# Chunk 1 of a fused mLSTM and feed-forward kernel: the next step's preparation handed over behind the joint products

## The chip, the core and the metric

The kernel runs on one core of one Trainium2 chip. The metric is device time in microseconds (us). The core has a matrix engine (TensorE, PE in the profile, with its weight loads shown apart as PEld), a vector engine (VectorE, DVE), a scalar engine (ScalarE, ACT), a general engine (GpSimd, POOL) and a sequencer that only issues transfers here (SyncE, SP). Each engine works through its own instructions in a fixed order and waits where one of them needs something that is not there yet. Transfers between memory and the on-chip buffers are issued by a queue and run beside the engines.

## The reference

Two blocks are computed, one after the other, in float32. The first is an mLSTM cell over 4 batches, 8 heads, 768 tokens and a head width of 40. At each token a decayed matrix state takes in one outer product, and the query reads it:

```python
m_new = np.maximum(f_gate[:, :, t] + m, i_gate[:, :, t])
C = f_stab * C + i_stab * einsum('bhd,bhe->bhde', vt, kt)
n = f_stab * n + i_stab * kt
h_tilde = einsum('bhde,bhe->bhd', C, qt)
y[:, :, t] = sigmoid(o_gate[:, :, t]) * h_tilde / maximum(abs(n . qt), 1.0)
```

The second takes y as 3072 tokens of width 320 through a feed-forward pair: `h = x @ w_in` (320 to 2048), `g = maximum(0.01 * h, h)`, `g @ w_out` (2048 to 320). The two weight matrices arrive as 64-bit floats and are narrowed to 32 bits on the chip.

## The kernel before, in words

The 768 tokens are cut into 6 chunks of 128. A step `s` is one chunk of one batch, so that chunk c holds steps 4c to 4c+3. In this document **step 4 to step 7** are the four steps of chunk 1, which alone the change touches. The recurrence inside a chunk is replaced by matrix products over two halves of 64 tokens, with one carried state per batch, kept in `S_t[s % 4]`.

The first chunk is written out (`first_chunk`). From then on a loop runs the feed-forward units of the chunk before (`ffs`, line 946 on) and sets the cell's work of the current chunk between them. In chunk 1 there are 30 units, i = 0 to 29. Units 0 to 13 are halves of the first product (line 743, `ph`, about 2.25 us of PE each), and units 14 to 29 are quarters of the second (line 778, `po`, about 2.2 us each). The tuple `place` (line 940) says behind which unit each of the cell's pieces stands. For the steps 4 to 7 there are two pieces, or visits:

- `u_parts(s)`, the first visit: it turns the scaled query (`split_qs`, line 504, `tq`), finishes the exponentials that are left, and makes the joint products, which are the scores and the state's increments in one pair of PSUM banks `sd0` and `sd1` (lines 598 and 603). VectorE then multiplies the scores by the decays (line 608, `qn`) and adds the first increment (line 580).
- `u_plain(s)`, the second visit, three units later: `prep_o` (line 478), the values `hN` (line 649), on POOL the decay of the state's second half (`state_next(s, 1)`, line 576), on VectorE the denominators and the gate (lines 617 to 660), on POOL the product at line 665, and on VectorE the second increment (`state_add(s, 1)`, line 580).

They stand behind units 2 and 5 for step 4, 7 and 10 for step 5, 12 and 15 for step 6, 18 and 21 for step 7. Behind unit 16 stands `u_gates(2)` (lines 312 and 317, `tg`).

The preparation of a step is `ahead(s)` (line 821). For the steps of chunk 1 it issues, in this order: `u_split(s)`, which turns the keys and the queries on PE (64 small products at line 518 into the PSUM pair `tk0`, `tk1`) and copies them out on ACT (four copies, line 524, `kqT`); the list of eight exponentials (line 442), of which three are run with each following unit; `prep_qs(s)` on POOL (line 471, `y<-rb`); the load of the queries of step s + 2 on SP (line 366, or line 382 and the spread of line 405 from step 8 on); `state_next(s, 0)` (line 576) and `prep_vu(s)` (line 462) on POOL; and `prep_mask(s + 1)` on POOL (line 434, `w<-w,i`), which adds the causal mask to the decays `w` of the step after.

What `ahead(s)` reads arrives by transfers of the SP queue: the keys (line 340, `kn`), the values (line 343), the decays (line 397, `w<-a_dr`, two transfers), the queries (line 366, `rb<-in_q_dram`) and the output gates. The order of that queue is fixed when the program is built. SP gives its transfers eight completion counters in turn, so that each issue first waits until the transfer eight places ahead of it has landed. Between them stand the loads of the weights (lines 213 and 218).

Meanwhile `narrow_weights` (lines 231 to 247) narrows the remaining weights, one operation on ACT and six on VectorE for each piece, some with each unit.

PSUM is given out in two groups of four banks: `mm` for `ph` and `po`, and `c` for the cell's pieces (`tq`, `tk`, `sd`, `hN`, `tg`). A piece gets a bank when the piece that held it has been read.

The order on PE, VectorE, ACT and POOL is that of the calls, since the whole runs under a manual schedule.

Of the kernel before, what the change touches and what calls it, by code (L numbers as in the profile page):

```python
# [18 lines left out]
def kernel(  # L19
# [27 lines left out]
    B, H, S, D = q.shape  # L47
# [140 lines left out]
    def load_weights(n):  # L188

        m = n - QN  # L190
        if n < QN:
            dst = w_in[:, n, :]
        else:
            dst = w_out[:, 2 * m : 2 * m + 2, :].rearrange("p a d -> p (a d)")
        to = dst
        if wide:
            if n < 2:
                at = NF * GT - 2 * WC * (n + 1)
                raw = acts_l[:, at : at + 2 * WC].bitcast(U64)
            elif n < QN:  # L200
                raw = raw_t[:, WC * (n - 2) : WC * (n - 1)]
            elif m < 2:
                raw = w_out[:].rearrange("p f d -> p (f d)")[:, (2 + m) * WC : (3 + m) * WC].bitcast(U64)
            else:
                at = (4, 0, 1, 2, 3, 4)[m - 2] * HW
                raw = raw_t[:, at : at + HW]
            raws[n] = (raw, dst)
            to = raw
        if n < QN:
            src = moe_w_in[:, n * QC : (n + 1) * QC].rearrange("(k p) (r c) -> r p k c", p=DP, r=2)  # L210
            for slot in range(KC):
                for r in range(2):
                    nc.sync.dma_start(  # L213
                        to[DP * r : DP * (r + 1), 2 * P * slot : 2 * P * (slot + 1)], src[r, :, SLOTS[r][slot], :],
                    )
        else:
            rows = moe_w_out[2 * m * P : 2 * (m + 1) * P, :]
            nc.sync.dma_start(to.rearrange("p (a d) -> p a d", d=Dm), rows.rearrange("(a p) d -> p a d", p=P))
# [142 lines left out]
    def load_late(s, i):  # L361

        if B <= s < 2 * B:
            if i > 0:
                c, b = divmod(s, B)
                nc.sync.dma_start(natural(s, i), (k, q, o_gate)[i][b, :, ts(c, P), :].rearrange("h p d -> p h d"))
        elif s < NS:
            load_blocks(s, i)
# [60 lines left out]
    def prep_mask(s):  # L429
        if s in masked:  # L430
            return
        masked.add(s)
        w = st[s]["w"]
        nc.gpsimd.tensor_tensor(w, w, cm2.unsqueeze(1).to_broadcast([P, H, SL]), op=ALU.add)  # L434
# [367 lines left out]
    def cell_units(c):  # L802
        if c == 1:
            units = [(fn, c * B + n) for n in range(B) for fn in (u_parts, u_plain)]
            units.insert(2 * B - 2, (u_gates, c + 1))
            return units + [(u_x, s) for s in range(B, 2 * B)]
        units = [(fn, c * B + n + m) for n in range(0, B, 2) for fn in (u_parts, u_mix) for m in range(2)]
        if c + 1 < NB:
            units.insert(2 * B - 2, (u_gates, c + 1))
        return units  # L810
# [5 lines left out]
    def run(steps, n=None):  # L816

        for _ in range(H if n is None else n):
            next(steps, None)
# [23 lines left out]
    def feed(s):  # L843
        load(s)
        spread(s)

    def first_chunk():

        for n in range(B):
            load(n)  # L850
        load_o(0)
        load_o(1)
        load_weights(0)
        load_o(2)
        load_o(3)
        for n in range(1, 3):
            load_weights(n)
        gates(0)
        gates_exp(0)
        warm(14)  # L860
        bu, a, _ = bus[0]
        gates_T(0, bu)
        u_transpose(0)
        spread_first(a, 0)
        run(prep_exp(0))
        prep_vu(0)
        prep_vu(1)
        prepare_tiles()
        u_transpose(1)
        u_scores(0)  # L870
        u_state(0)
        run(prep_exp(1))
        spread_first(a, 2)
        gates(1)
        gates_exp(1)
        u_scores(1)
        u_values(0)
        u_state(1)
        u_transpose(2)
        prep_o(0)  # L880
        gate(0)
        run(prep_exp(2))
        prep_vu(2)
        w = narrow_weights(0)
        next(w, None)
        u_values(1)
        u_gates(1)
        u_scores(2)
        prep_o(1)
        gate(1)  # L890
        u_state(2)
        for _ in w:
            pass
        u_transpose(3)
        run(prep_exp(3))
        prep_vu(3)
        prepare_step(0)
        prepare_step(1)
        u_x(0)
        u_values(2)  # L900
        u_scores(3)
        u_x(1)
        u_state(3)
        prep_o(2)
        gate(2)
        w = narrow_weights(1)
        for _ in range(4):
            next(w, None)
        ffs = ff_units(0)
        ffs[0]()  # L910
        u_values(3)
        prep_o(3)
        gate(3)
        u_x(2)
        ffs[1]()
        for _ in w:
            pass
        u_x(3)
        prepare_step(2)
        prepare_step(3)  # L920
        return ffs

    E = mybir.EngineType
    with tc.manual_schedule(engines={E.PE, E.DVE, E.Activation, E.Pool}):
        ffs = first_chunk()
        for s in (B, B + 1):
            feed(s)
            for i in range(1, 3):
                load_late(s, i)
            if s == B:  # L930
                load_weights(3)
        for n in range(3):
            load_weights(QN + n)
        for s in (B + 2, B + 3):
            feed(s)


        ffs = ffs[2:]
        fetch = {4: (3, 4), 8: (5, 6), 15: (7,)}
        place = (2, 5, 7, 10, 12, 15, 16, 18, 21, 22, 24, 26, 28)  # L940
        late = {}
        masks = {0: (2, 3), 12: (4, 5)}
        pairs = (2, 2, 6, 6, 14, 14, 19, 19, 19)
        now = (None for n in range(2, QN + NF // 2) for _ in narrow_weights(n))
        for c in range(1, NB + 1):
            if c > 1:
                ffs = ff_units(c - 1)
            cells = cell_units(c) if c < NB else []
            n_ff, n_c = len(ffs), len(cells)
            done = fed = 0  # L950
            waiting = []
            for i in range(n_ff):
                if c == 1:
                    run(now, 2 if i < 10 else 3 if i < 14 else 4)
                    for n in fetch.get(i, ()):
                        load_weights(QN + n)
                    if i == 0:
                        prep_mask(B)
                        ahead(B)
                        load_fi(3)  # L960
                for s, steps in lazy.items():
                    if s in late and late[s] > 0:
                        late[s] -= 1
                    else:
                        run(steps, 3)
                for n in masks.get(i, ()) if 1 < c < NB else ():
                    if c * B + n < NS:
                        prep_mask(c * B + n)
                ffs[i]()
                if c + 1 < NB:  # L970
                    if i == (1 if c == 1 else 0):
                        gates(c + 1)
                    if i == (3 if c == 1 else 2):
                        gates_exp(c + 1)
                upto = min(n_c, sum(p <= i for p in (place if c == 1 else pairs)))
                while done < upto:
                    fn, s = cells[done]
                    fn(s)
                    done += 1
                    if fn is u_mix:  # L980
                        waiting.append(s)
                    if fn is u_plain and s < 2 * B - 1 or fn is u_parts and s == 2 * B - 1:
                        ahead(s + 1)
                    elif fn is u_mix:
                        ahead(s + 2)
                    elif fn is u_plain:
                        prep_mask(s + 2)
                        ahead(s + 2)
                if i >= n_ff // 2 - 1:
                    for s in waiting:  # L990
                        gather_x(s)
                    waiting.clear()
                while fed < done:
                    fn, s = cells[fed]
                    fed += 1
                    if fn in (u_mix, u_plain):
                        load_late(s + NR, 2)
                        if s + NL < NS:
                            feed(s + NL)
# [31 lines left out]
```

## Time and profile before

| | |
|---|---|
| median of 3 runs | 528.49 us (528.32 to 528.70) |
| the profiled execution's own time | 528.25 us |
| its span, first to last instruction | 526.4 us |
| PE busy | 513.2 us (97%) |
| DVE, ACT, POOL busy | 240.3, 168.1, 113.0 us |
| mean granted PE clock | 0.976 |

The profile covers one execution. Its span is 1.85 us shorter than that execution's time, and its time is 0.24 us below the median. Times in the lines are from the start of the span. A line of the timeline gives start, length, engine, source line, operation and output<-inputs; a bracket at its end tells how long the engine sat idle before it and what ended that. SPq is the issuing of a transfer, and its length is that of the issue, not of the transfer.

### The profile page before, as it was taken

To read this page: it belongs to the slowest core of one execution; us is meant where nothing else is said; L and a number is where in the kernel's file an instruction comes from. 1 tells how busy PE (TensorE), PEld (TensorE's weight loads), DVE (VectorE), ACT (ScalarE), POOL (GpSimd) and SP (SyncE) were. 2 spreads that over 40 slices of the span, in tenths; PEclk is the share of its full clock that TensorE was granted. 3 is DMA by queue.
4 is the path that set the end of the run, shared out by engine and by line. 5 is a ranking of instruction groups with operands and counts; after the bars stand their busy time and mean duration, and the time that the engine had idled before them with its cause. 6 is when DMAs were issued, how large, how long until landed. Compare 5 with 4: busy or idle time off the path is not lost.

```text
span 526.4 us, 11333 instructions
## 1 busy us (share of the span) xinstructions
PE 513.2 (97%) x4501; PEld 336.3 (64%) x4501; DVE 240.3 (46%) x431; ACT 168.1 (32%) x458; POOL 113.0 (21%) x145
## 2 busy tenths in 40 slices
PE   8889989999999999999999999999999999999997
PEld 7877878777555577555577555577554577544675
DVE  4679998999328446028445028344028230000000
ACT  4565865534534212034212124212125100122100
POOL 4244354152205121015021015021013010000000
PEclk9668999999999999999999999999999999999999
DMA  9977687888755626685626676626542112000000
GB/s 116 156 204 153 138 212 171 196 145 175 146 137 105 137 72 150 129 174 107 138 75 143 134 150 129 138 76 155 125 102 52 50 52 87 14 0 1 12 12 25
DMA packets 165284, 59.13 MB, mean 112 GB/s; under 512 B 128816, under 2 KB 156016, under 8 KB 165232
## 3 DMA queue, kind: packets, MB, share of 16 engines
q1 hardware_dynamic: 164848, 58.28, 51.0%
q8 instruction: 35, 0.57, 0.5%
q10 hardware_dynamic: 384, 0.13, 0.1%
q14 instruction: 17, 0.14, 0.1%
HBM read 51.68 MB, written 6.70 MB: 111 GB/s over the span
## 4 chain that ended last, share of the span: by engine, by line
PE 83%; SPq 6%; DVE 4%; DMA 2%; ACT 2%; issue 1%; POOL 1%; ACTq 0%; POOLq 0%
PE po L778 38%; PE ph L743 36%; PE pT L679 3%; SPq L213 3%; PE sd L598 3%; SPq L338 2%; SPq L352 1%; PE sd L603 1%; DMA rb<-in_q_dram 1%; DVE raw L245 1%; DVE qn L608 1%; DMA S<-in_v_dram 0%; DMA raw<-in_moe_w_in_dram 0%; PE tk L518 0%; PE hN L649 0%
## 5 line engine op out<-in xcount | busy, mean ns | idle before, releaser
L743 PE MATMUL ph<-xT,w_in 64*128 64x512 f32 (+1 forms) x1120 | 215.2, 536 | 0.6 <-ACT acts L751 0.6
L778 PE MATMUL po<-w_out,acts 128*128 128x320 f32 x768 | 211.1, 434 | 0.0
L778 PEld LDWEIGHTS po<-w_out,acts 128*128 128x128 f32 x768 | 144.5, 190 | 62.6 <-issue 4.1
L743 PEld LDWEIGHTS ph<-xT,w_in 64*128 64x128 f32 x1120 | 107.8, 189 | 94.4 <-issue 87.7
L751 ACT ACTIVATE acts<-ph 128x512 f32<-128x512 f32 (+1 forms) x112 | 53.9, 534 | 151.8 <-PE ph L743 151.7
L608 DVE TENSOR_TENSOR qn<-w,sd 64x512 f32<-64x512 f32 x40 | 27.4, 684 | 97.7 <-PE sd L603 57.1
L576 POOL TENSOR_TENSOR S<-S,f 40x336 f32<-40x336 f32 x36 | 30.9, 858 | 101.9 <-PE pT L679 65.8
L442 ACT ACTIVATE w<-w,gT 128x64 f32<-128x64 f32 (+1 forms) x192 | 51.1, 348 | 3.1 <-POOL w L434 2.1
L434 POOL TENSOR_TENSOR w<-w,i 128x512 f32<-128x512 f32 x20 | 28.1, 1411 | 104.7 <-ACT bu L294 53.0
L786 ACT COPY y<-po 128x320 f32<-128x320 f32 x12 | 5.1, 423 | 83.3 <-PE po L778 83.3
L786 ACT COPY hn<-po 128x320 f32<-128x320 f32 x12 | 5.1, 426 | 76.0 <-PE po L778 76.0
L686 DVE STREAM_TRANSPOSE hb<-pT 128x512 f32<-128x512 f32 x16 | 11.4, 714 | 39.2 <-PE pT L679 39.0
L495 DVE TENSOR_TENSOR qn<-kqT,ea 64x512 f32<-64x512 f32 x32 | 27.3, 854 | 0.9
L693 POOL TENSOR_TENSOR xb<-xb,den 128x320 f32<-128x320 f32 x16 | 11.7, 728 | 66.5 <-DVE xb L690 66.5
L598 PEld LDWEIGHTS sd<-kqT 40*64 40x64 f32 x640 | 19.9, 135 | 6.1 <-issue 6.1
L697 DVE STREAM_TRANSPOSE x<-xb 128x512 f32<-128x512 f32 x16 | 18.1, 1130 | 7.7 <-POOL xb L693 7.7
L598 PE MATMUL sd<-kqT 40*64 40x64 f32 x640 | 21.5, 220 | 0.0
L603 PE MATMUL sd<-S,vu 64*40 64x42 f32 x576 | 20.1, 214 | 0.7 <-POOL vu L462 0.7
L489 DVE STREAM_TRANSPOSE kqT<-rb 128x512 f32<-128x512 f32 x32 | 20.5, 677 | 0.0
L603 PEld LDWEIGHTS sd<-S,vu 64*40 64x40 f32 x576 | 18.6, 111 | 0.8 <-POOL vu L462 0.8
L580 DVE TENSOR_TENSOR S<-S,sd 40x336 f32<-40x336 f32 x36 | 18.1, 503 | 1.0
L679 PEld LDWEIGHTS pT<-qn,S 128*64 128x64 f32 x512 | 15.6, 138 | 3.6 <-issue 3.5
(126 smaller groups left out, 364.9 us busy)
## 6 DMA issues: line engine op xcount, KB each, us to landing
w<-a_dr SPq DMA_DIRECT2D x40, 128.0 KB
rb<-in_k_dram SPq DMA_DIRECT2D x64, 80.0 KB
rb<-in_q_dram SPq DMA_DIRECT2D x64, 80.0 KB
rb<-in_o_gate_dram SPq DMA_DIRECT2D x64, 80.0 KB
ea<-a_dr SPq DMA_DIRECT2D x32, 128.0 KB
kn<-in_k_dram SPq DMA_DIRECT2D x24, 160.0 KB
raw<-in_moe_w_out_dram SPq DMA_DIRECT2D x6, 640.0 KB
S<-in_v_dram SPq DMA_DIRECT2D x80, 40.0 KB
```

Of the source, the lines that this page charges most:

```text
L434: nc.gpsimd.tensor_tensor(w, w, cm2.unsqueeze(1).to_broadcast([P, H, SL]), op=ALU.add)
L442: yield nc.scalar.activation(w[:, h, :], w[:, h, :], AF.Exp, bias=gT[c][:, 0, bh : bh + 1], scale=1.0)
L489: nc.vector.transpose(d["kqT"][:, i].rearrange("p (h t n) -> p h n t", n=TS, t=QW), raw_blocks(s, i, QW).rearrange("p (h n) d -> p h n d", ...
L495: nc.vector.tensor_tensor(mixed(s)[rows, 1 - r], d["kqT"][rows, 1].rearrange("p (h t) -> p h t", t=SL), d["ea"][rows], op=ALU.mult,)
L576: nc.gpsimd.tensor_tensor(new, old, g, op=ALU.mult)
L598: nc.tensor.matmul(bank[1 - u][toks, h, :], lhsT=kqT[rows, 0, ts(h, SL)], rhs=kqT[rows, 1, ts(h, SL)], start=True, stop=True,)
L603: nc.tensor.matmul(dC[u][:, h].rearrange("p k d -> p (k d)"), lhsT=d["ku"][toks, h], rhs=S_v[s % NL][toks, u, h, :, :V1], start=True, stop ...
L608: nc.vector.tensor_tensor(mixed(s)[toks, u], w[toks], bank[1 - u][toks], op=ALU.mult)
L679: nc.tensor.matmul(pT[DP * r : DP * (r + 1), j * P + u * SL : j * P + (u + 1) * SL], lhsT=S[:, u, h, :], rhs=m[:, u, h, :], start=True, st ...
L743: nc.tensor.matmul(ph[r][:, cols], lhsT=w_row(r, slot, j), rhs=xT[DP * r : DP * (r + 1), slot, cols], start=(slot == 0), stop=(slot == KC ...
L751: nc.scalar.activation(acts[:, f, cols], ph[r][:, cols], AF.Prelu, alpha=0.01)
L778: nc.tensor.matmul(po[n][:], lhsT=acts[:, f, ts(n, P)], rhs=w_out[:, f, :], start=(f == 0), stop=(f == NF - 1),)
```

## The change

In chunk 1 `ahead(s + 1)` is called behind `u_parts(s)` and no longer behind `u_plain(s)`, for s = 4, 5 and 6. Nothing else is different: step 8 was already prepared behind `u_parts(7)`, and step 9 with its mask is still prepared behind `u_plain(7)`.

```diff
-                    if fn is u_plain and s < 2 * B - 1 or fn is u_parts and s == 2 * B - 1:
+                    if fn is u_parts and s < 2 * B:
                         ahead(s + 1)
                     elif fn is u_mix:
                         ahead(s + 2)
-                    elif fn is u_plain:
+                    elif fn is u_plain and s == 2 * B - 1:
                         prep_mask(s + 2)
                         ahead(s + 2)
```

So the preparations of steps 5, 6 and 7 are issued three units earlier, behind units 2, 7 and 12 where they were behind 5, 10 and 15. In the built program the same instructions stand on every engine. On PE the 64 small products of line 518 move ahead of three units and of `hN` of the step before; on ACT their four copies and the exponentials move with them; on POOL the preparation's four instructions, the mask of the step after among them, move ahead of the step before's lines 576 and 665; VectorE's order is unchanged. On SP the queries of step 7 move ahead of eight issues, the queries of step 8 (four transfers) and the loads before them ahead of two weight loads, and some neighbours change places. The queries of steps 5 and 6 stay where they were in SP's order, since the calls that load them (before the loop, and `ahead(4)` at unit 0) are not moved.

## The prediction

> **What bounds the kernel now.** I read first the page's busy times and its chain.
>
> ```profile
> PE 513.2 (97%) x4501; PEld 336.3 (64%) x4501; DVE 240.3 (46%) x431; ACT 168.1 (32%) x458; POOL 113.0 (21%) x145
> PE 83%; SPq 6%; DVE 4%; DMA 2%; ACT 2%; issue 1%; POOL 1%; ACTq 0%; POOLq 0%
> ```
>
> PE is busy for 513.2 of 526.4 us and carries 83% of the chain. An edit that adds and removes no PE work can only act through PE's idle time. So I cut the span into stretches (columns: stretch, length, busy time of PE, PEld, DVE, ACT, POOL, granted PE clock, DMA share, GB/s).
>
> ```profile
> 62.00:72.00 10.00, 10.00 (x172) 8.78 (x170) 9.80 (x10) 5.88 (x15) 3.07 (x2) 1.00 0.96 267
> 72.00:80.00 8.00, 6.37 (x134) 5.43 (x132) 7.09 (x11) 5.58 (x17) 5.66 (x5) 1.00 0.71 92
> 80.00:90.00 10.00, 10.00 (x170) 8.78 (x170) 8.36 (x16) 5.39 (x13) 3.06 (x4) 1.00 0.68 191
> 100.00:110.00 10.00, 9.31 (x127) 6.71 (x126) 9.63 (x16) 5.59 (x14) 5.06 (x5) 1.00 1.12 244
> 140.00:526.00 386.00, 383.22 (x2930) 229.80 (x2926) 125.17 (x231) 86.99 (x241) 59.22 (x69) 1.00 0.40 93
> ```
>
> Steps 4 to 7 lie between 50 and 125 us. There PE is idle for 1.63 us (72 to 80) and 0.69 us (100 to 110), and DVE is nearly as full as PE. Behind 140 us PE idles 2.8 us in 386, so a delay made earlier isn't given back. The view of waits, PE alone, 52 to 140 us, names these holes:
>
> ```profile
> PE tq L504 <- POOL y L471: 0.9, 1, 0.9
> PE tg L312 <- DVE hn L660: 0.7, 1, 0.7
> PE sd L603 <- POOL vu L462: 0.7, 1, 0.7
> PE ph L743 <- ACT acts L751: 0.6, 1, 0.6
> ```
>
> The first and third are step 5's own preparation on POOL, late. They are what an earlier handing over can win: 0.94 + 0.69 = 1.63 us.
>
> Then I asked whether the inputs of the moved work are there three units earlier. PE's timeline gives where the splits would stand, SP's when their queries are issued.
>
> ```profile
> 50.59 0.25 PE L518 MATMUL tk<-ident,rb 64*40 64x64 f32 x2 [0.34 <-DMA rb<-in_q_dram]
> 61.37 6.75 PE L743 MATMUL ph<-xT,w_in 64*128 64x256 f32 x60
> 68.05 1.13 PE L649 MATMUL hN<-S,qn 128*64 128x42 f32 x32
> 70.14 4.59 PE L743 MATMUL ph<-xT,w_in 64*128 64x256 f32 x40
> 78.64 6.75 PE L743 MATMUL ph<-xT,w_in 64*128 64x256 f32 x60
> 46.84 0.58 SPq L366 DMA_DIRECT2D rb<-in_q_dram  x1
> 61.29 0.58 SPq L366 DMA_DIRECT2D rb<-in_q_dram  x1
> 72.84 2.10 SPq L397 DMA_DIRECT2D w<-a_dr  x2
> 80.79 0.54 SPq L366 DMA_DIRECT2D rb<-in_q_dram  x1
> ```
>
> Step 4's queries are issued at 46.84 and PE waits for them until 50.59. Those of step 5 are issued at 61.29, of step 6 at 80.79. From the completion marks of each transfer in the trace, which no view lists, I take the landings: step 4's queries 50.54, step 5's 65.31, step 6's 83.97; step 6's decays `w` 77.02 and 78.43, step 7's 81.74 and 83.43; step 5's keys 59.57, step 6's 73.75. The splits now start at 69.1 and 86.4, 2 to 4 us behind the landings. The change puts them at 61.37 and 78.64: ahead of both.
>
> [...] The edit makes the wait earlier and leaves the two issues in place[...] here 0.58 us shown against 3.70 to the landing. [...] This trace has such drops to 0.50 in its first 44 us, each lasting a multiple of 3.41 us, and none after. [...] Line 471 here takes 0.72 to 1.97 us for the same work, so POOL's sums carry about 1 us of doubt.
>
> **The change part by part.** Nothing is added or removed; the cost is in order. The clock is before's.
>
> *Split of step 5, behind unit 2.* PE is through with the joint products of step 4 at 61.37. Its two key products of the first head can start; the first query product waits until 65.31 + 0.05. Stall 3.99 us. The 64 products take 1.03 us (69.11 to 70.14), so units 3, 4, 5 start at 66.4. Queued behind the wait on ACT are the copies of line 524, then a `w_in` piece (1.36), three exponentials (0.82) and the relu of unit 3: 66.55 + 2.35 + 1.36 + 0.82 + 0.66 = 71.75. Unit 5 wants that relu's bank at 70.9, a stall of 0.8 (such a wait, 0.6 us, is the fourth row above). `hN` of step 4 starts near 73.7, units 6 and 7 end near 79.3, `tq` of step 5 at 80.4.
>
> *POOL.* The mask of step 6 now stands before line 576 of step 4. It waits for `w` at 78.43 and takes 1.27; then line 576 takes 0.9, to 80.7. VectorE's line 580 waits for that, to 81.3, with all narrowing queued behind it (before: 72.86). `sd0` of step 5 takes the bank which that line 580 reads, so PE stalls about 0.9 us, and the joint products of step 5 end near 82.3. The two waits of 1.63 us are gone: lines 471 and 462 of step 5 are done by 71.
>
> *Split of step 6, behind unit 7.* PE arrives at 82.3 and the queries land at 83.97. This landing makes the detail above immaterial: whatever PE lost before, unit 8 starts at 83.97 + 0.05 + 1.03 = 85.05 instead of 78.64. That is 6.41 later, with 1.03 us of split already done: **5.38 us net**.
>
> *Split of step 7, behind unit 12.* Its queries move ahead of eight issues, to about 82.5, and land near 86, well ahead of 99. But `tk1` now takes the bank of `tq1`, which ACT must first copy out. In step 4 that copy ends 2.3 us after `tq` starts (59.42 to 61.73), the joint products end after 1.95: stall 0.4 us.
>
> *`tg`.* Its bank was the one read by line 660; in the new order it is `tk0`'s, free long before. The 0.69 us wait goes.
>
> *VectorE's backlog.* From line 580 of step 5 (88.02) to that of step 7 (119.63) VectorE runs almost without a hole, and PE comes to `hN` of step 7 at 119.76, just behind. In the new order `hN` of step 5 ends at 92.9, the same stretch starts at 94.5, and without its 0.9 us of holes ends at 125.2, against PE's arrival at 124.7: stall 0.5 us.
>
> *SP.* From 62 to 84 us its issues wait only for transfers and for work of chunk 0, so the two landings don't move with PE. The weight loads that move back by ten issues (about 5 us) feed narrowing that has slipped as much.
>
> *Clock.* [...] at most 3.41 us at half speed, up to 1.7 us of PE time. If one window, it ends before 83.97 and the landing hides it; uncovered it costs that 1.7. The second hole, about 1.5 us, is shorter than PE's hole of 1.8 us at 40.11, which stands in a stretch at 0.50; I take 0.2 for it, between 0 and 1.7.
>
> Sum: 5.38 + 0.4 − 0.69 + 0.5 + 0.2 = **5.8 us**. Span 526.4 + 5.8 = 532.2; profiled time 528.25 + 5.8 = 534.05; against the median, 528.49 + 5.8 = **534.3 us**.
>
> **The rivals.**
>
> *A, faster.* The splits find their queries landed, and the three waits of 0.94, 0.69 and 0.69 us go: 528.49 − 2.3 = 526.2 us. It decides if queries land by 61.4 and by about 77. For it: the waits are real and of the kind named. Against it: the second is issued at 80.79. A gain needs the stalls to sum to less than 2.3 us; the first alone is 3.99.
>
> *B, only the first landing counts.* If step 6's queries came by 79, what is left is 3.99 + 0.8 + 0.4 − 1.63 − 0.69 = 2.9: 531.4 us. The DMA share of 0.71 in 72 to 80 leaves some room, but SP's own issues are the pace there.
>
> *C, VectorE becomes the bound.* It stands still from 65.1 to 70.3 (for the `w_in` piece behind ACT's copies) and from 77.7 to 80.8 (line 580): 8.3 us, against 4.3 idle in all between 62 and 110 before. If the narrowing then falls 2 to 4 us further behind PE, `hN` and the last quarters of the second product wait for it; two windows at half clock would come to the same size. 8 to 9.5 us: 536.5 to 538 us.
>
> *D, no difference*: the stalls and the three waits cancel. For that the first landing would have to come 1.7 us earlier and the second not to count.
>
> **How the numbers follow.** My forecast 0.70, A 0.03, B 0.12, C 0.13, D 0.02. A measurement of this kernel can tell about 0.2% (1.06 us) from no change. So faster 0.03, same 0.02, slower 0.95. The forecast's own range is 4.6 to 7.2 us (the clock's 0 to 1.7, POOL's doubt, landings moving by some tenths): 533.1 to 535.7. To hold 8 in 10 I reach into B and C: 532.0 to 537.0.
>
> **What would show it.** In the new profile: PE idle about 4 us ahead of line 518 near 61.4, ended by the transfer of `rb`, and 1 to 2 us again ahead of the second split, ended near 84; no wait of `tq` or `sd` for lines 471 and 462; POOL's line 576 of step 4 near 80 instead of 69.3; no wait of `tg` for line 660; behind 140 us the same stretches as before, all later by one amount. The prediction is wrong if PE's idle time between 52 and 140 us grows by less than 3 us, or if PE finds queries landed at either split.

## The result, and the profile after

The changed kernel takes 533.51 us (median of 5 runs, 532.02 to 534.49) against 528.63 us (528.32 to 529.55) for the kernel before on the same chip: a ratio of 1.0088, interval 1.0070 to 1.0107. The change costs about 4.9 us. The time forecast, 534.3 us in a range of 532.0 to 537.0, holds. The way to it does not hold in every part, and the profile says so at once. Its execution took 532.02 us and has a span of 530.2 us, 3.8 more than before. First the busy times and the chain of the page after:

```profile
PE 517.6 (98%) x4501; PEld 339.7 (64%) x4501; DVE 236.9 (45%) x431; ACT 168.8 (32%) x458; POOL 111.4 (21%) x145
...
PE 84%; SPq 8%; DMA 3%; issue 1%; ACT 1%; DVE 1%; POOL 1%; ACTq 0%; POOLq 0%
```

The same instructions keep PE 4.4 us longer busy, so in this execution PE did not stand still longer, it ran slower for a while (granted clock 0.69 in the first 50 us, 0.76 before). The stretches after (length, busy PE, PEld, DVE, ACT, POOL, granted clock, DMA share, GB/s):

```profile
72.00:80.00 8.00, 8.00 (x152) 6.86 (x153) 4.55 (x9) 4.40 (x13) 2.75 (x3) 1.00 0.59 111
80.00:90.00 10.00, 9.36 (x185) 8.01 (x176) 9.67 (x14) 7.34 (x22) 3.90 (x4) 1.00 0.75 195
100.00:110.00 10.00, 10.00 (x78) 7.03 (x74) 8.05 (x16) 7.77 (x19) 0.82 (x1) 1.00 0.94 214
140.00:530.00 390.00, 386.97 (x2945) 232.23 (x2943) 125.14 (x231) 89.56 (x247) 57.92 (x68) 1.00 0.40 92
```

The two stretches with holes before, 72 to 80 and 100 to 110, are full now; the hole has gone to 80 to 90, and behind 140 us all is as before. PE's waits after, 50 to 146 us (total, times, longest):

```profile
PE ph L743 <- ACT acts L751: 1.6, 2, 1.3
PE tk L518 <- DMA rb<-in_q_dram: 0.6, 1, 0.6
PE tk L518 <- issue: 0.6, 1, 0.6
PE tk L518 <- ACT qn L506: 0.5, 2, 0.3
```

The waits for lines 471, 462 and 660 are gone, 2.32 us in all. In their place stand one wait for queries, 0.62 us within the second split, and several others at line 518. The stall of 3.99 us that I had put ahead of the first split is not there. The timeline of PE after (start, length, and in the bracket the idle time before):

```profile
59.17 2.70 PE L743 MATMUL ph<-xT,w_in 64*128 64x256 f32 x20 [1.25 <-ACT acts L751]
...
64.16 0.25 PE L518 MATMUL tk<-ident,kn 64*40 64x64 f32 x1 [0.23 <-ACT qn L506]
...
70.14 2.70 PE L743 MATMUL ph<-xT,w_in 64*128 64x256 f32 x20 [0.37 <-ACT acts L751]
...
81.63 0.25 PE L518 MATMUL tk<-ident,rb 64*40 64x64 f32 x2 [0.62 <-DMA rb<-in_q_dram]
...
97.60 0.25 PE L518 MATMUL tk<-ident,kn 64*40 64x64 f32 x1 [0.30 <-ACT qn L506]
```

The reason lies ahead of the change. In the trace's record of the clock PE had half its clock from 20.36 to 47.67 us without a break; in before's execution it had 3.41 us of full clock within that time and was at full speed from 44.20 on. So PE came to `tq` of step 4 at 61.80 us (before: 59.42), in code that is the same in both (0.66 of these 2.38 us are a longer wait for a relu, 1.25 us against 0.59), and to the first split at 63.66, when the queries had landed at 63.25. A late PE had taken the place of the stall. Whether that, or the wait for queries, or something else makes the 4.9 us, one profile can't tell.

I began with three theories. **T1**: the end is set where PE meets the landing of step 6's queries, and PE's start-up does not matter. **T2**: the start-up alone makes the difference. **T3**: the new order costs by itself, by ACT's copies ahead of the relus, POOL's mask ahead of line 576, VectorE's backlog.

### The profile page after: what moved, and what is told of

It reads as the page before. It is cut to its first block, busy times and chain, and to the rows that moved or that the text cites. A ratio compares the mean times of both kernels' runs of the same rounds, so it can differ in the third digit from the quotient of the medians.

```text
span 530.2 us, 11331 instructions
## 1 busy us (share of the span) xinstructions
PE 517.6 (98%) x4501; PEld 339.7 (64%) x4501; DVE 236.9 (45%) x431; ACT 168.8 (32%) x458; POOL 111.4 (21%) x145
## 4 chain that ended last, share of the span: by engine, by line
PE 84%; SPq 8%; DMA 3%; issue 1%; ACT 1%; DVE 1%; POOL 1%; ACTq 0%; POOLq 0%
PE po L778 40%; PE ph L743 36%; PE pT L679 3%; SPq L213 3%; PE sd L598 3%; SPq L338 2%; SPq L343 1%; SPq L352 1%; DMA w_out<-in_moe_w_out_dram 1%; PE sd L603 1%; PE hN L649 1%; SPq L397 1%; DMA rb<-in_q_dram 1%; DMA raw<-in_moe_w_in_dram 0%; DMA acts<-in_moe_w_in_dram 0%
```

## The experiments

**Both kernels once more.** No edit.

> The kernel before once more, for a second profile of it. Two executions already profiled (one of before, one of after) differ by about 2.4 us at 60 us, in code that both share: in the second PE was granted half its clock from 20.36 to 47.67 us, in the first it had 3.41 us of full clock within that stretch, and SP's transfers landed 2 us earlier in the second. Theory T1 (the landing of step 6's queries sets the end of after, and PE's start-up doesn't): before's time moves with PE's start-up, after's with the landing, so a profile of before with a late start-up should show its whole time later by as much. Theory T2 (the start-up alone makes the difference): before shows times from 528 to 531 or 532 according to its start-up. In both, ratio 1.000; T2 is favoured if the several times of before spread over 2 us or more, T1 if they stay within 1.3 us as so far (528.32 to 529.55) while those of after lie 3 to 6 us above.

> The changed kernel once more, for a second profile. T1: the second split (line 518 before unit 8) is ended by the landing of step 6's queries, and unit 8 starts about 1.1 us behind that landing, whatever PE's start-up was; time 532 to 535. If PE's start-up is the early one (full clock in a stretch between 34 and 38 us), then PE waits 2 to 4 us at the first split as predicted and 0.5 to 2 us at the second. T2: with the early start-up the time falls to 529 to 530. T3 (the order itself costs: ACT's copies ahead of the relus, POOL's mask ahead of line 576, VectorE's backlog): no wait for transfers worth over 1 us at either split, time 532 to 534 all the same.

The kernel before: 528.46 us (527.03 to 530.02, 20 runs). The changed kernel: 532.73 us (530.27 to 534.67, 14 runs), ratio 1.0077 (1.0060 to 1.0095) to 528.36 us (49 runs). With more runs the two ranges meet at their ends (the longest of those 49 runs of the kernel before took 530.74 us), but start-up does not explain the gap: T2 falls with the profile, where PE reaches `tq` of step 4 at 57.75 us in before's second profile and at 58.03 in after's, and the spans are still 526.4 and 530.5. PE's waits between 50 and 100 us in that second profile after:

```profile
PE tk L518 <- DMA rb<-in_q_dram: 3.1, 1, 3.1
PE tk L518 <- ACT qn L506: 0.8, 3, 0.3
PE ph L743 <- ACT acts L751: 0.6, 1, 0.6
```

And its timeline:

```profile
63.77 0.33 PE L518 MATMUL tk<-ident,rb 64*40 64x64 f32 x2 [3.08 <-DMA rb<-in_q_dram]
...
65.64 8.65 PE L743 MATMUL ph<-xT,w_in 64*128 64x256 f32 x60
74.22 1.01 PE L649 MATMUL hN<-S,qn 128*64 128x42 f32 x27
```

Here is the stall of the forecast, 3.08 us, ended by the transfer of `rb`. The 60 products behind it take 8.65 us where they took 6.75 before, since the clock was halved from 62.70 to 69.53. That is twice 3.41 us, the step in which the clock records of both first profiles change (a window from here on). The two profiles pair as follows. A row is how much later than in its pair of the kernel before PE reaches the piece (first profiles of both, then second profiles of both), less the 1.03 us of a split already done where the orders differ.

| PE comes to | forecast | first pair | second pair |
|---|---|---|---|
| `tq` of step 4 | 0 | +2.38 | +0.28 |
| unit 3 | +4.0 | +2.8 | +4.9 |
| `tq` of step 5 | +4.7 | +2.7 | +5.8 |
| end of step 5's joint products | +3.7 | +1.8 | +4.1 |
| unit 8 | +5.4 | +3.0 | +5.0 |
| `tq` of step 6 | +5.4 | +3.0 | +3.9 |
| unit 13 | +5.8 | +4.5 | +4.8 |
| unit 17 | +5.1 | +3.7 | +4.1 |
| span's end | +5.8 | +3.8 | +4.1 |

From 2.4 and 0.3 us at the start the pairs come to 3.8 and 4.1 at the end. What binds them is at unit 8. By the completion marks in the trace, step 6's queries land at 81.59 and 82.49 us, and unit 8 starts 1.06 and 1.07 us behind. The issue of these queries and the products of unit 8, in the first profile and then in the second:

```profile
78.15 0.53 SPq L366 DMA_DIRECT2D rb<-in_q_dram  x1
82.65 6.75 PE L743 MATMUL ph<-xT,w_in 64*128 64x256 f32 x60
...
79.33 0.53 SPq L366 DMA_DIRECT2D rb<-in_q_dram  x1
83.56 6.75 PE L743 MATMUL ph<-xT,w_in 64*128 64x256 f32 x60
```

That speaks for T1. (The second profile of before itself loses 0.6 us at half clock in step 5's joint products and 1.0 us between unit 8 and `hN` of step 5, which is why the second pair drops there.)

**The query loads earlier.** If only landings count, loading the queries sooner must give the loss back. In the changed kernel, and as a control in the kernel before, step 5's queries are issued ahead of a whole piece of `w_in` (ten transfers) and of step 5's own keys, values and decays. The keys, values and decays of steps 6 and 7 (`feed`) are issued behind step 6's queries, which `ahead(4)` issues at unit 0:

```diff
-                load_late(s, i)
+                if s == B or i > 1:
+                    load_late(s, i)
             if s == B:
+                load_late(B + 1, 1)
                 load_weights(3)
...
-        for s in (B + 2, B + 3):
-            feed(s)
...
                         ahead(B)
+                        feed(B + 2)
+                        feed(B + 3)
```

> The change, with the query loads ahead: on SP the queries of step 5 are issued ahead of the three weight loads, and those of step 6 at unit 0 ahead of the keys, values and decays of steps 6 and 7. The compute order is that of after. T1: the queries have landed at both splits, line 518 waits for no transfer; what is left is the relu behind ACT's copies (0.4 to 0.8), the bank of tk1 at step 7 (0.4 to 1.4), and a gain of 0.94 + 0.69 + 0.69 for the waits that go: 527 to 529 us, ratio 0.997 to 1.001 to before. T3: most of the loss stays, 531 to 533. The loads moved back (keys and decays of step 6) may become the new wait: then line 518 waits for kn, or POOL's line 434 for w and PE behind it, and the time lies between.

> Control: the same order of loads on the kernel before. T1 and T3: no wait of before is for the queries of steps 5 and 6 (its splits stand 2 to 4 us behind the landings), so nothing is won: 528 to 529 us, ratio 0.999 to 1.001; a loss would be the price of loading keys and decays later.

The control: 528.16 us, 0.9994 (0.9981 to 1.0007), as expected. The changed kernel: 534.11 us, 1.0102 (1.0068 to 1.0136), no better at all. T1 as I had put it falls. The queries landed at 52.33 and 73.43 us, and PE met another wait. PE's waits in this kernel:

```profile
PE sd L598 <- DVE S L580: 4.6, 1, 4.6
PE ph L743 <- ACT acts L751: 1.7, 1, 1.7
PE tk L518 <- DMA rb<-in_q_dram: 1.0, 1, 1.0
...
```

(The third stands at 50 us, ahead of the change's place.) The chain behind the first, from the timeline of this kernel:

```profile
79.24 1.26 POOL L434 TENSOR_TENSOR w<-w,i 128x512 f32<-128x512 f32 x1 [8.17 <-DMA w<-a_dr]
80.58 0.77 POOL L576 TENSOR_TENSOR S<-S,f 40x336 f32<-40x336 f32 x1
...
81.38 0.51 DVE L580 TENSOR_TENSOR S<-S,sd 40x336 f32<-40x336 f32 x1 [7.24 <-POOL S L576]
...
81.94 0.37 PE L598 MATMUL sd<-kqT 40*64 40x64 f32 x1 [4.63 <-DVE S L580]
```

Step 6's decays land at 79.08, the mask runs to 80.5, line 576 of step 4 stands behind it on POOL, VectorE's line 580 of step 4 waits for that, and PE for the bank that line 580 reads. How long PE waits there hangs on one more landing: these decays came at 76.48 and 77.46 us in the two profiles of the changed kernel. From the landing to the end of the wait it is 2.86 us, and PE came at 77.31, so with decays at 76.48 the wait would be about 2.0 us and not 4.63. That is an estimate from these figures, not a run. In the two profiles of the changed kernel the same chain ran, and was hidden. The first profile after, its timeline on POOL and VectorE:

```profile
76.60 1.26 POOL L434 TENSOR_TENSOR w<-w,i 128x512 f32<-128x512 f32 x1 [7.74 <-DMA w<-a_dr]
77.94 0.76 POOL L576 TENSOR_TENSOR S<-S,f 40x336 f32<-40x336 f32 x1
...
78.74 0.51 DVE L580 TENSOR_TENSOR S<-S,sd 40x336 f32<-40x336 f32 x1 [3.28 <-POOL S L576]
```

Line 580 ended at 79.25, and PE came to the joint products of step 5 at 79.28. So the theory became **T4**: the change puts three waits for transfers in a row (queries of step 5, decays of step 6 through POOL, queries of step 6), and taking one away leaves the others.

**The mask back, with and without the early loads.** The mask of the step after goes back behind the second visit, behind lines 576 and 665:

```diff
-            if s + 1 <= 2 * B:
+            if s == B:
                 prep_mask(s + 1)
...
-                    elif fn is u_plain and s == 2 * B - 1:
+                    elif fn is u_plain:
                         prep_mask(s + 2)
-                        ahead(s + 2)
+                        if s == 2 * B - 1:
+                            ahead(s + 2)
```

> Theory T4, formed on the run with early query loads (line 518 waited for almost nothing there, but PE then waited 4.6 us ahead of line 598 for line 580, itself held by POOL's line 576 behind the mask of step 6, whose decays w landed at 79.1): the change puts three waits for transfers in a row, the queries of step 5, the decays of step 6 through POOL, and the queries of step 6, and the last of them to be over sets the end. Here the query loads are ahead and the mask of step 6 (7, 8) is back behind the second visit, behind lines 576 and 665. T4: no wait of over 1 us for a transfer or for line 580; the waits of 0.94, 0.69 and 0.69 us are gone, 0.4 to 0.8 for a relu and 0.4 to 1.4 for the bank of tk1 come in: 526.5 to 528.5 us, ratio 0.996 to 1.000. T3 (the order on ACT and VectorE costs by itself): 530 or more.

> The change with only the mask of the step after put back behind the second visit; the query loads stay where they are. T4: the queries of step 6 still land at 81.5 to 84 and set unit 8, so the time stays within 1 us of the changed kernel's 532.7: 531.7 to 533.5. If POOL's order alone were the cause (T5), it falls to 529 or less.

With both edits: 528.06 us, 0.9997 (0.9981 to 1.0012). The whole loss is given back. With the mask alone: 533.27 us, 1.0080 (1.0054 to 1.0106), nothing given back, since the queries of step 6 still landed at 81.80 and unit 8 started at 82.87, again 1.07 behind:

```profile
81.84 0.25 PE L518 MATMUL tk<-ident,rb 64*40 64x64 f32 x2 [1.98 <-DMA rb<-in_q_dram]
...
82.87 8.43 PE L743 MATMUL ph<-xT,w_in 64*128 64x256 f32 x60
```

Here one window at half clock (82.98 to 86.39) adds 1.7 us behind the landing. So neither edit does it alone, and both together do: this is T4 shown, and T5 (POOL's order alone) and the larger part of T3 refused. PE's waits with both edits:

```profile
PE ph L743 <- ACT acts L751: 1.0, 2, 0.7
PE tk L518 <- ACT qn L506: 0.8, 3, 0.3
PE tk L518 <- issue: 0.7, 1, 0.7
```

Of these 2.4 us (0.97, 0.76 and 0.66), 0.28 stands at 55 us, ahead of the change's place. The other 2.1 are the order's own price, and it eats what the three lost waits (2.32 us) bring.

**One step at a time.** The call is moved for one step alone (shown for step 5, the others alike):

```diff
-                    if fn is u_parts and s < 2 * B:
+                    if fn is u_parts and s + 1 in (5, 2 * B):
                         ahead(s + 1)
+                    elif fn is u_plain and s < 2 * B - 1 and s + 1 != 5:
+                        ahead(s + 1)
```

> Only step 5's preparation is handed over behind the joint products. T4: PE waits 3 to 4 us at the first split for the queries; then line 580 of step 4, held by the mask of step 6, makes sd0 of step 5 wait 0.5 to 2 us; 1.63 us of old waits go; 0.5 to 1.5 for a relu and the clock: +2.5 to +4, 531 to 532.5 us. Rival: step 6's landing alone makes the loss, then within 1 us of before.

> Only step 6's preparation is handed over behind the joint products. T4: PE comes to that split at its time of before, 77.6 to 78.6 us, and waits for queries that land at 81.5 to 84: unit 8 starts 4 to 5.4 us later net of the split, and the clock may drop behind so long a hole (0 to 1.7): +4 to +6, 532.5 to 534.5 us, about the whole of the loss. Together with the run of step 5 alone the two exceed the whole change, since in it the first stall lies within the second. Rival: the first stall alone makes the loss, then within 1 us of before.

> Only step 7's preparation is handed over behind the joint products of step 6. Its queries then land well ahead of the split. T4: the wait of tg for line 660 (0.69) goes, the bank of tk1 and the copies ahead of it cost 0.8 to 1.5 (the split took 1.6 to 2.5 us in the runs so far, against 1.04): 528.0 to 529.5 us, ratio 0.999 to 1.002. Rival: the whole loss comes from this one, 531 or more; a gain of 0.7 would show that the bank costs nothing.

| moved | us | ratio (interval) | against the kernel before beside it |
|---|---|---|---|
| step 5 alone | 532.19 | 1.0058 (1.0044 to 1.0073) | +3.9 |
| step 6 alone | 534.07 | 1.0095 (1.0065 to 1.0125) | +5.7 |
| step 7 alone | 528.97 | 1.0018 (1.0004 to 1.0032) | +0.9 |
| all three | 532.73 | 1.0077 (1.0060 to 1.0095) | +4.4 |

The three sum to 10.5, the whole is 4.4: the first stall makes PE late for the second, as T4 says. By the medians step 6 alone costs more than all three, though the two intervals overlap. PE's waits in the run of step 6 alone:

```profile
PE tk L518 <- DMA rb<-in_q_dram: 5.4, 2, 4.4
PE tq L504 <- POOL y L471: 0.9, 1, 0.9
PE sd L603 <- POOL vu L462: 0.7, 1, 0.7
```

And PE's timeline behind the hole:

```profile
84.04 8.60 PE L743 MATMUL ph<-xT,w_in 64*128 64x256 f32 x60
```

A hole of 4.38 us, from 77.80 to 82.18, comes with two windows at half clock (81.00 to 87.83): the split takes 1.9 us behind the landing instead of 1.1, and the 60 products 8.60 instead of 6.75. In step 7's run the wait for line 660 went and line 518 took 1.6 us instead of 1.0; so these two account for about none of its +0.9 us. Its execution (529.61 us) also had a window at half clock from 77.94 to 81.35, ahead of the place of this change, behind the same two waits as in the second profile of before. Whether that is chance, or has a part in the median, I leave open.

**What the change could have won, taken without the rest.** In the kernel before, three of step 5's instructions on POOL are issued behind unit 3, and nothing else is moved; then, besides, the gates' products stand behind unit 17:

```diff
                 ffs[i]()
+                if c == 1 and i == 3:
+                    prep_qs(B + 1)
+                    state_next(B + 1, 0)
+                    prep_vu(B + 1)
...
-        place = (2, 5, 7, 10, 12, 15, 16, 18, 21, 22, 24, 26, 28)
+        place = (2, 5, 7, 10, 12, 15, 17, 18, 21, 22, 24, 26, 28)
```

(`ahead(5)` leaves these three out; the second hunk is in the second kernel only.)

> The kernel before, with three of step 5's instructions on POOL (line 471, line 576, line 462) issued behind unit 3, ahead of line 576 of step 4, and nothing else moved: the split and the mask stay. T4: these are what the change could win. Line 471 starts as the queries land (64 to 65.3) and ends before 67, so the waits of PE for lines 471 and 462 (0.94 + 0.69 = 1.63) go, and with them the chance of a clock drop behind them (as in the second profile of before, 76.24 to 79.65 us): 526.5 to 527.5 us, ratio 0.996 to 0.999. Rival: the wait only moves on (VectorE's lines 608 or 580, or a relu), 528 to 528.7.

> The same, and the products of lines 312 and 317 behind unit 17 where they stood behind unit 16, 2.2 us further from line 660, whose bank they take. T4: the wait of 0.69 us goes too: 525.8 to 526.8 us, ratio 0.995 to 0.998. Rival: the next chunk's gates come too late and the wait stands elsewhere; then as the run before this one, or slower.

The first: 526.76 us, 0.9980 (0.9966 to 0.9993), 1.35 us less than the kernel before beside it: a small gain, but its interval leaves out 1. Its timeline on POOL:

```profile
65.30 1.30 POOL L471 TENSOR_TENSOR y<-rb,gT 128x320 f32<-128x320 f32 x1
66.68 1.89 POOL L576 TENSOR_TENSOR S<-S,f 40x336 f32<-40x336 f32 x1
68.65 1.19 POOL L462 TENSOR_TENSOR vu<-kn,gT 128x320 f32<-128x320 f32 x1
69.92 1.89 POOL L576 TENSOR_TENSOR S<-S,f 40x336 f32<-40x336 f32 x1
```

The three run while PE is in units 3 to 5, and line 576 of step 4 follows at 69.92 (before: 69.31). No wait for line 471 or 462 is left. Part of the gain goes to the next wait in the row: PE now comes to the second split at 82.77, before its queries (83.42), and stays there 0.7 us longer than the split takes.

The second: 531.80 us, 1.0078 (1.0060 to 1.0097), the rival's side. The wait of 0.69 us goes, and a larger one comes. PE's waits in that kernel:

```profile
PE sd L598 <- DVE f L324: 3.2, 1, 3.2
...
```

VectorE's timeline ahead of the end of that wait:

```profile
110.89 0.49 DVE L243 TENSOR_SCALAR raw<-w_out 128x640 uint32<-128x640 uint32 x1
111.42 0.83 DVE L245 SCALAR_TENSOR_TENSOR raw<-raw 128x640 f32<-128x640 uint32 x1
112.28 0.23 DVE L322 COPY gT<-tg 128x64 f32<-128x64 f32 x1
112.42 0.21 DVE L324 COPY f<-tg 128x64 f32<-128x64 f32 x1
```

The copies that free the gates' bank stand in VectorE's order behind the narrowing, and run at 112.28 although the products began at 105.35. The joint products of step 7 wanted that bank, and two half-clock windows (111.58 to 118.40) come with the wait.

**Both good edits together**: the three POOL instructions early and the query loads early.

> The kernel before with both edits that were measured apart: three of step 5's instructions on POOL behind unit 3, and the query loads of steps 5 and 6 ahead in SP's order. In the run of the first alone PE came to the second split at 82.8 us, 2.4 us earlier than in the second profile of before, and then waited 1.6 and 0.3 us there for queries (landed 83.42 and later). T4: with those landed at about 72 us these waits go too: 0.3 to 1.5 us better than the 526.8 of that run, 525.3 to 526.5 us, ratio 0.994 to 0.997. Rival: the loads that move back (decays of step 6 and 7) or another wait takes its place, 526.5 to 528.5.

526.98 us, 0.9979 (0.9959 to 0.9998). It is not told apart from the kernel without the early loads. Line 518's wait for queries is gone there, but its execution waited 1.25 us for a relu ahead of `tq` of step 4, as the first profile after did without early loads, and 0.5 us at `po` for line 247. Whether the early loads have a part in the second I did not settle.

## Why the prediction was right, and where not

**The time**: right, by a mechanism that was right in kind. The splits come ahead of their queries, and unit 8 hangs on the second landing: 1.08 us behind it by the forecast, 1.06, 1.07 and 1.07 in three profiles. It is too high by 0.9 us against the first comparison and by about 1.4 against the longer one (4.4 lost instead of 5.8). These 4.4 us lie below the forecast's own range of 4.6 to 7.2 and inside the wider one. One premise was too narrow: that an edit without PE work can act only through PE's idle time. In both profiles of the changed kernel the clock had a part, ahead of the change in the first (half from 20.36 to 47.67 us) and at the stall in the second (half from 62.70 to 69.53).

**The landing, 83.97 us: mis-sized, and the main error.** I read it from one execution and let it stand as fixed. It is 81.59 and 82.49 in the two profiles of the changed kernel, 81.80 with the mask back, and in the two kernels before 83.97 and 81.81. So "5.38 us net" measured 3.0 and 5.0. A spread of 2.4 us belonged in the range; I gave landings "some tenths". The landing followed its issue: issued at 80.79 in before's first profile and at 78.15 and 79.33 in the two of the changed kernel, 3.18, 3.44 and 3.16 us from issue to landing. What shifts the issue I did not settle.

**First stall, 3.99 us**: 0 and 3.08 (0.85 with the mask back, 4.05 in the run of step 5 alone). It is the difference of two times that both vary: PE's arrival between 59.9 and 63.7, the landing between 63.02 and 65.31. My two tests, that PE's idle time between 52 and 140 us grows by 3 us or more and that PE finds no queries landed, both failed in the first profile: idle time grew from 2.92 to 3.45 us, and the first queries lay ready. In the second pair the idle time grew by 2.0 us (2.55 to 4.54), again too little, and neither set of queries lay ready. By these words the prediction would be wrong, although its time held. The test should have been the slip of unit 8 behind the landing, not idle time, which a late PE or a half clock hides.

**The relu, 0.8 us**: 0.37 in the first profile, none listed in the second, 0.69 with early loads and mask back, 1.67 with early loads alone. Right in kind.

**POOL's mask**: right in every link (line 576 of step 4 at 77.94 and 78.92 us, forecast about 79.8; VectorE's line 580 held 3.28 and 3.35 us), and hidden in the changed kernel as "makes the detail above immaterial" said. But I priced it at 0.9 us with the cover and gave no price without it. Uncovered it was 4.63 us and two half-clock windows (granted clock 0.66 from 80 to 90 us), in an execution in which the decays landed at 79.08, against 78.43 in before and 76.48 and 77.46 in the changed kernel. One figure on the way is wrong by the forecast's own steps: where units 6 and 7 end at 79.3, `tq` of step 5 follows at once, and 80.4 is about its end. So the table's +4.7 in that row should read +3.6; the joint products' end at 82.3 is not touched.

**The bank of `tk1`, 0.4 us**: the split of step 7 took 2.4 and 1.8 us instead of 1.0, so 0.8 to 1.4. The line named, ACT's copies, is right (0.30 in each profile), and does not cover it all.

**The wait for line 660, −0.69 us**: right. Unit 17 against unit 13 in the table: −0.7 and −0.8.

**VectorE's backlog, 0.5 us**: not there. The waits between 50 and 146 us list none for VectorE in either profile. (PE's arrival of 124.7 in that term comes to 124.85 by the sum's own parts, which makes the stall 0.35.)

**The clock, 0.2 us**: 3.41 us is the first drop in before's record (13.48 to 16.89); that the first hole would bring one such drop was my estimate. In the first profile there was none in chunk 1 (full clock from 47.67 us on). In the second a drop of two windows (62.70 to 69.53), not one, and the landing then covered it, as said: PE came to the second split at 81.65, the queries at 82.49.

**The rivals.** B, only the first landing counts, is refused by the run of step 6 alone (+5.7 us). C, VectorE as the bound, is refused by the missing waits. A supposed that both splits find their queries, at 526.2 us. That was made true: it gave 534.11 us, and with the mask back 528.06. D, no difference, is refused by the ratio. A left out the mask's chain and the 2.1 us at a relu and at line 518, so its gain of 2.3 us was never to be had by this route.

## What to carry to other kernels

When work is moved ahead, list every transfer that its instructions wait for on every queue, and give each its arrival and its price as if the other waits were gone: here three stood in a row, and taking two of them away gave nothing (534.11 us). A landing time, or a stall, read from one execution is a difference of two varying times; read it in several before it carries a forecast. And move only what the profile shows waiting: three POOL instructions gave 1.35 of the 2.3 us for which the whole preparation had been moved.

## What the runs showed of the hardware

**When the clock dropped.** In the clock records of the first profiles of both kernels the granted clock is full or half (1.00 or 0.50), and each change stands a whole number of windows of 3.41 us behind the one before. I cut these two executions into windows and summed PE's idle time in each. Between 46 and 515 us the most idle windows held 1.44 us (before, from 74.92) and 1.25 us (changed kernel, from 57.90), and full clock followed both. In the second profile of before, 1.64 us in one window was followed by half clock. In the run with early loads alone, a wait of 1.67 us up to 67.90 was not (granted clock 1.00 from 60 to 80 us); whether it lay in one window is not shown. In the last 12 us of the spans PE runs line 778 without a break and then has no more work. There a window with 1.87 us idle in the changed kernel (from 525.43) was not followed by half clock, and one with 2.26 us in before (from 522.07) was. (This drop, at 525.48 us, is missing where the forecast says that there is none behind 44 us.) Ahead of 46 us, where PE's work is of other kinds, windows with 0.33 and 0.74 us idle in before (from 16.89 and 33.96) were also followed by half clock. So no single idle time parts the two in these runs, and what sets the drop is not shown.

In before's first profile an edge at 74.92 us cut 0.19 us off the two waits of 0.94 and 0.69 us, the window behind it held 1.44 us, and the clock stayed. In the second profile both waits fell into one window, 1.64 us, and the clock dropped. The second profile's stretches:

```profile
62.00:72.00 10.00, 10.00 (x170) 8.80 (x168) 9.73 (x12) 6.54 (x18) 3.37 (x4) 1.00 0.96 257
72.00:84.00 12.00, 10.36 (x156) 8.78 (x156) 9.92 (x13) 5.95 (x18) 5.38 (x5) 0.86 0.55 103
84.00:100.00 16.00, 16.00 (x280) 13.07 (x277) 12.97 (x21) 10.75 (x27) 6.32 (x6) 1.00 0.87 223
```

Half clock stood from 76.24 to 79.65 and cost 1.6 us: 0.6 from `tq` of step 5 to unit 8 (3.56 us against 2.97 in the first profile) and 1.0 from unit 8 to `hN` of step 5 (7.68 against 6.68). So a pair of waits of 1.63 us cost 3.2 in this execution. A hole of 1.98 us, with the mask back, was followed by one window (82.98 to 86.39), 1.7 us in the 60 products behind it (8.36 us against 6.68). Single holes of 3.08, 3.20, 4.05, 4.38 and 4.63 us came with two windows in all five runs that had one. Behind three of them (3.08, 4.05 and 4.38 us) the split and the 60 products took 2.0 to 2.7 us longer.

**How much one kernel varies in start-up.** PE reached `tq` of step 4 between 57.75 and 61.80 us over the 14 profiled executions, in code that no experiment changed apart from the order of loads. The kernel before took from 526.75 to 530.74 us over all its runs. A single execution can't tell kernels apart that differ by less.
